# Four edits in an attention-and-feed-forward kernel: spare matmuls ahead of the first transposes, column-index steps moved, a group's work moved, one batch's second product taken by halves

## The chip, the cores and the metric

The kernel runs on one NeuronCore of one Trainium2 chip. The metric is the device time of one execution in microseconds (us). The kernel before takes 352.08 us (median of 3 runs, 351.84 to 352.71).

Names of engines, as the profile has them: PE is the matrix engine and PEld its weight load; DVE, ACT and POOL are the vector, scalar and general engines; SP is a queue that here only issues DMAs. POOL issues DMAs too. Each engine and each queue works through its own list in order; semaphores order them against each other.

## What is computed

```python
# attention: q, k, v of (8 batches, 8 heads, 576 tokens, 64), 8 global tokens, window 32
scores = 1/sqrt(D) * q @ k.T
mask = abs(i - j) <= 32  or  i is global  or  j is global
attn = softmax(where(mask, scores, -1e9))
x = attn @ v                      # -> (4608, 512)
# feed-forward with 2048 hidden columns
h = x @ w_in
g = h + sin(alpha * h)**2 / (alpha + 1e-9)
out = g @ w_out                   # (4608, 512), float32
```

## The kernel before

The eight batches go through three stages, which overlap. **Attention** of batch b (`attention_first` for b = 0, `attention` for the others) takes the four pairs of heads `hp` in turn: scores into the PSUM tile `ring` (L843, L975), exponential on ACT into `E` (L850, L984), mask on DVE (L851, L985), then two products on PE, the sums of the weights (`OB` or `ones`) and the weighted values (`VD` or `VX`), at L882 or L1013; ACT makes the inverse `R` of the sums, DVE multiplies into `xT` (L901, L1031). **gemm1** of batch b makes 16 groups `nt` of 128 hidden columns: eight matmuls with `w_in` (L1172) into one of three PSUM tiles `zn`, `zr`, `zd`, sine on ACT (L1211), square on ACT or DVE (L1214, L1216), and the sum into `H` on DVE (L1217). **gemm2** multiplies `H` by `w_out` (L1266) in blocks of 128 tokens, 16 matmuls to a block, into the two PSUM tiles `zo`; ACT copies each block out and SP stores it. gemm2 of batch b is a generator: `fill(n)` takes its next n matmuls and puts them on PE between the instructions of attention b+1 and of gemm1 of batch b+1 (tables `START`, `FIRST`, `SECOND`, `PER_GROUP` and so on). So the order on each engine is written out by hand, and PE's matmuls run in that order whatever is ready.

Names that the steps below use:

- `turn_part` (L625) transposes the first keys and queries, loaded into parts of `H2` (shown as `H`), by matmuls of 48 columns into `zn`, `zd`, `zo`; `place_part` copies them to `KD` (ACT) and `QX` (DVE). `warm(z, n)` (L576) puts n matmuls of 512 columns of ones on PE whose result is not read.
- `load_lying` (L458) loads keys and queries of batch 1 as they lie, in four DMAs of POOL; `turn_lying` (L733) transposes them in thirds at groups 2, 6 and 9 of gemm1 of batch 0 into both `zo` tiles, and `place_lying` copies them out one group later (DVE to `KX`, L741; ACT to `QX`, L747).
- `turn_kq` (L773, L777) turns the global rows of all batches (`gq`, `gk`, loaded by SP's gathers, L518) into `kTg` and `qTg`, by way of the same `zo` tile. `cast_globals_v` (L765, POOL) makes `VGb` from the gathered `gv`; `place_globals` puts global columns into batch 1's `KX` and `QX`; `load_vg` (L422) and `load_v` (L418) are SP's loads of batch 1's values into `VX`.
- `find_columns` (L1231 to L1243) is seven DVE instructions on 8 or 16 numbers: from the global indices it makes the column numbers `gcol`. They are read in attention 5 by `load_columns`.
- `beside(at)` is called after pair `at` of an attention and holds its side work: `place` (L362, L369), DVE copies of the next batch's keys and queries, and, from batch 2 to batch 5 at pair 2, `pace` (L347), which holds POOL until the first pair's `xT` stands, and then POOL's casting loads of the batch after next (`cast_qk`, L336, and `cast_v`, L343).

Of the kernel before, what the change touches and what calls it, by code (L numbers as in the profile page):

```python
# [249 lines left out]
def kernel(  # L250
# [12 lines left out]
    B, H, S, D = q.shape  # L263
# [8 lines left out]
    NT = DFF // P  # L272
# [72 lines left out]
    def pace(src):  # L345

        nc.gpsimd.tensor_copy(out=seen[0 : src.shape[0]], in_=src)  # L347
# [117 lines left out]
    zo = [banks.tile([P, 512], DT.float32, name=f"zo{i}") for i in range(2)]  # L465
# [108 lines left out]
    def warm(z, n):  # L574
        for _ in range(n):
            nc.tensor.matmul(  # L576
                out=z[:], lhsT=ones[:], rhs=ones[:][:, None, :].to_broadcast([P, 4, P]),
                start=True, stop=True, skip_group_check=True,
            )
# [41 lines left out]
    def turn_part(w, half, z):  # L621
        part[w, half] = z
        rows = slice(D * half, D * half + HK)
        for a in range(NH):
            nc.tensor.transpose(  # L625
                out=z[a // 12][:, a % 12], in_=nat[w][rows, a * P : (a + 1) * P], identity=identb[rows, rows]
            )

    def views(zs):
        return [z.bitcast(DT.bfloat16)[:, 0 : NH // 2 * HK].rearrange("p (a c) -> p a c", c=HK) for z in zs]  # L630
# [32 lines left out]
    def place_global_queries(t, copy):  # L663
        for y in range(2):
# [4 lines left out]
                ].to_broadcast([D, NHP, 7, 4]),  # L669
            )  # L670

    turn_part(1, 0, views([zn[:, n, :] for n in range(2)]))
    for n in range(2):
        place_part(1, 0, n, act)
    turn_part(0, 0, views([zd[:, n, :] for n in range(2)]))

    gpf = setup.tile([P, 1], DT.float32, name="gpf")
    nc.vector.tensor_copy(out=gpf[:], in_=gp64[:].bitcast(DT.int32)[:, 0:1])
# [110 lines left out]
    def halves(z, W):  # L789
        c = columns(z, W)  # L790
        return [(c[:, lo:hi], lo, hi) for lo, hi in ((0, HALF), (HALF, W))]
# [281 lines left out]
    def global_rows(bs):  # L1073

        nc.vector.reciprocal(out=GR[:, :, :, bs], in_=GD[:, :, :, bs])
# [78 lines left out]
    def gemm1(b):  # L1154


        while len(waiting) > 1:
            fill(1)
        xT = xTs[b]
        r0 = (b % 2) * S  # L1160
        more = b == B - 1
        W = SG if more else S
        hr = tc.alloc_tile_pool(name="hr", bufs=1, space=PSUM)
        hs = {}

        def chunks(nt, cs, parts=slice(0, 2)):
            if nt not in hs:
                hs[nt] = (zn, None, zd)[nt % 3] or hr.tile([P, 2, 512], DT.float32, name="zr")
            h = hs[nt]
            for c in cs:  # L1170
                for h_part, lo, hi in halves(h, W)[parts]:
                    nc.tensor.matmul(  # L1172
                        out=h_part, lhsT=w_in[:, c, nt * P : (nt + 1) * P], rhs=xT[:, c, lo:hi],
                        start=(c == 0), stop=(c == CT - 1), skip_group_check=True,
                    )

        on_act = (ON_ACT_FIRST, ON_ACT_SECOND, ON_ACT)[min(b, 2)]
        for nt in range(NT):
            at_group[0] = (b, nt)
            if b == 1 and nt in (10, 12):  # L1180
                for which, t, y in PLACES[nt - 6 : nt - 4]:
                    place(2, which, t, y, nc.vector.tensor_copy)
            if b == 0 and nt in (3, 7, 10):
                for w, copy in ((1, nc.vector.tensor_copy), (0, nc.scalar.copy)):
                    place_lying(w, (3, 7, 10).index(nt), copy)
            if b == 0 and nt == 4:
                turn_kq()
            if b == 0 and nt == 5:

                cast_globals_v()  # L1190
                for part in range(3):
                    place_globals(1, part, nc.gpsimd.tensor_copy)
                load_vg(1)
                load_v(1)
            if more and nt == SOON:
                put_globals(slice(0, SOON))
            if nt == 0:

                for n in range(2):
                    chunks(n, range(CT - 1), slice(0, 2 - more))  # L1200
                for n in range(2 * more):
                    chunks(n, range(CT - 1), slice(1, 2))
            chunks(nt, range(CT - 1, CT) if nt < 2 else range(CT))
            h = columns(hs[nt], W)
            fill((GROUP_LAST if more else PER_GROUP)[nt])
            if nt and copied[0] == (b, nt - 2):
                fill(AFTER_COPY)
            if b == 0 and nt in (2, 6, 9):
                turn_lying((2, 6, 9).index(nt))
            sb = spool.tile([P, SG], DT.bfloat16, name="sb")  # L1210
            nc.scalar.activation(out=sb[:, 0:W], in_=h, func=AF.Sin, scale=alphaT[:, nt : nt + 1])  # L1211
            s2 = spool.tile([P, SG], DT.bfloat16, name="s2")
            if nt in on_act:
                nc.scalar.activation(out=s2[:, 0:W], in_=sb[:, 0:W], func=AF.Square)  # L1214
            else:
                nc.vector.tensor_tensor(out=s2[:, 0:W], in0=sb[:, 0:W], in1=sb[:, 0:W], op=ALU.mult)  # L1216
            nc.vector.scalar_tensor_tensor(  # L1217
                out=H2[:, nt, r0 : r0 + W], in0=s2[:, 0:W], scalar=recipT[:, nt : nt + 1], in1=h,
                op0=ALU.mult, op1=ALU.add,
            )  # L1220
        hr.release()
        at_group[0] = None
# [27 lines left out]
    SOON = 11  # L1250
# [7 lines left out]
    def gemm2(b):  # L1258
        lo, hi = (0, 4) if b % 2 == 0 else (4, 9)

        def bank(blk):
            return zo[(blk + b // 2) % 2]

        def products(blk, ops, nts, cols):
            for nt in nts:
                nc.tensor.matmul(  # L1266
                    out=ops[:, cols], lhsT=H2[:, nt, blk * P : (blk + 1) * P], rhs=w_out[:, nt, cols],
                    start=(nt == 0), stop=(nt == NT - 1), skip_group_check=True,
                )
                yield True  # L1270

        def keep(blk, ops, osb, cols):
            nc.scalar.copy(out=osb[:, cols], in_=ops[:, cols])  # L1273
            copied[0] = at_group[0]
            store(b, blk, osb, cols)

        full = slice(0, DM)
        if b == B - 1:
            for blk in (lo, lo + 1):
                yield from products(blk, bank(blk), range(SOON), full)  # L1280
        for blk in range(lo, hi):
            osb = osbp.tile([P, DM], DT.float32, name="osb")
            if (b, blk) == (B - 1, hi - 1):
                for part, ops in enumerate((bank(blk), zd[:, 1])):
                    cols = slice(part * DM // 2, (part + 1) * DM // 2)
                    yield from products(blk, ops, range(NT), cols)
                    keep(blk, ops, osb, cols)
            else:
                begun = SOON if b == B - 1 and blk < lo + 2 else 0
                yield from products(blk, bank(blk), range(begun, NT), full)  # L1290
                keep(blk, bank(blk), osb, full)

# [33 lines left out]
    def fill(n):  # L1326
        while n and waiting:
            if next(waiting[0], None) is None:
                waiting.pop(0)
            else:  # L1330
                n -= 1
# [15 lines left out]
    def phase_a(b_att, b_moe):  # L1347
        def beside(at):

            if b_moe is None:  # L1350
                if at == 0:
                    second_half()
                    gather(v, gv)
                if at == 2:
                    find_columns()
                if at == NHP:
                    for half in range(2):
                        rows = slice(half * D, (half + 1) * D)
                        nc.sync.dma_start(out=MASKT[rows], in_=MASK[rows, half * NT6 : (half + 1) * NT6])
                return  # L1360
            if at == 2 and b_att == B - 1:
                global_rows(slice(0, B - 1))
            if b_att == 5 and at == 3:
                load_columns()
            if 0 <= at < 2:
                square_x(b_moe, at)
            if at == 2 and 1 < b_att and b_att + 2 < B:
                pace(xTs[b_att][0:1, 0, 0:1])
                cast_qk(b_att + 2)
                cast_v(b_att + 2)  # L1370
            if b_moe == 0 and at == 1:
                turn_qk(2)
            for which, t, y in places_at(b_att, at):
                place(b_att + 1, which, t, y, nc.vector.tensor_copy)

        if b_moe is not None:
            waiting.append(gemm2(b_moe))
        attention(b_att, beside)
# [71 lines left out]
```

## Time and profile before

| | |
|---|---|
| median of 3 runs | 352.08 us (351.84 to 352.71) |
| span of the profiled execution | 351.6 us |
| PE busy | 324.5 us (92%) |
| ACT busy | 287.1 us (82%) |
| DVE busy | 276.1 us (79%) |
| POOL busy | 60.7 us (17%) |
| read and written in HBM | 41.97 MB, 20.77 MB |

All times inside the kernel are read from that one execution, counted from its start; its span stands 0.5 us under the median of the runs. A row of the timeline is: start, length, engine, line, operation, output and inputs, count of equal instructions, and in brackets how long the engine was idle before it and what ended the wait. A row of the windows gives, for a stretch of time, the busy time of each engine, the granted clock of PE as a share of full speed, the mean busy share of the 16 DMA engines as the page's own sum has it, and GB/s. PE's clock is known from the first change that the profile records, at 25.5 us; before that the column prints 1.00, and the lengths of the matmuls tell the clock.

### The profile page before, as it was taken

The numbers are of one execution on the slowest core, as the hardware profiler recorded it, in microseconds if no ns is written. First come the engines' busy times: TensorE is split into PE (matmuls) and PEld (weight loads), VectorE is DVE, ScalarE is ACT, GpSimd is POOL, SyncE is SP. The second block draws the span as 40 slices with busy tenths as digits, with TensorE's granted clock in tenths as the row PEclk, the third lists the DMA queues.
The fourth block names the chain that finished last, engine by engine and source line by source line (L and its number), as shares of the span: only waits on it lengthen the run. The fifth ranks groups of instructions, "written<-read, shape, count | busy, mean of one in ns | idle before, by whom it ended". The sixth has DMA issues, their size and how long they took to land.

```text
span 351.6 us, 10962 instructions
## 1 busy us (share of the span) xinstructions
PE 324.5 (92%) x4484; PEld 207.1 (59%) x4484; DVE 276.1 (79%) x537; ACT 287.1 (82%) x428; POOL 60.7 (17%) x93
## 2 busy tenths in 40 slices
PE   1576798999899999999999999999999999999994
PEld 1566575566645675567656674577556755566543
DVE  6787668778879887987878887978788878788970
ACT  6786778998979888988898888988898787887921
POOL 7966130024004000310003000400000000002510
PEclk9998889999999999999999999999999999999998
DMA  7999999479998957399428936799125011100142
GB/s 113 110 125 171 184 215 232 100 155 170 211 125 170 194 107 164 70 182 216 63 64 167 167 75 146 145 194 185 32 53 134 3 33 64 34 27 5 31 106 66
DMA packets 87762, 42.25 MB, mean 120 GB/s; under 512 B 72378, under 2 KB 82362, under 8 KB 87322
## 3 DMA queue, kind: packets, MB, share of 16 engines
q0 software_dynamic: 44944, 18.52, 44.1%
q1 hardware_dynamic: 42762, 22.98, 30.3%
q8 instruction: 36, 0.59, 0.7%
q14 instruction: 20, 0.16, 0.2%
HBM read 41.97 MB, written 20.77 MB: 178 GB/s over the span
## 4 chain that ended last, share of the span: by engine, by line
PE 43%; issue 29%; DVE 5%; ACT 3%; POOL 2%; POOLq 1%; DVEq 0%; ACTq 0%
PE zo L1266 21%; PE zn L1172 6%; PE zr L1172 5%; PE zd L1172 4%; PE ring L975 3%; DVE H L1217 2%; POOL H L1256 2%; PE zd L1013 2%; PE zn L1013 1%; POOLq L1248 1%; ACT sb L1211 1%; DVE xT L1031 1%; ACT s L1214 1%; DVE KD L369 1%; PE zd L1266 1%
## 5 line engine op out<-in xcount | busy, mean ns | idle before, releaser
L1266 PE MATMUL zo<-w_out,H 128*128 128x512 bf16 (+1 forms) x576 | 149.4, 377 | 0.2 <-POOL H L1256 0.2
L1172 PEld LDWEIGHTS <-w_in 128*128 128x128 bf16 x1024 | 99.8, 98 | 43.0 <-issue 8.2
L1266 PEld LDWEIGHTS <-H 128*128 128x128 bf16 x592 | 52.4, 98 | 44.3 <-POOL H L1256 0.7
L1172 PE MATMUL zn<-xT,w_in 128*128 128x288 bf16 (+1 forms) x384 | 57.3, 288 | 1.7 <-DVE H L1217 1.7
L1172 PE MATMUL zr<-xT,w_in 128*128 128x288 bf16 x320 | 48.7, 291 | 1.5 <-DVE H L1217 1.5
L984 ACT ACTIVATE E<-ring 128x720 bf16<-128x720 f32 x56 | 43.5, 776 | 7.6 <-PE ring L975 6.8
L1211 ACT ACTIVATE sb<-zn,alphaT 128x576 bf16<-128x576 f32 (+1 forms) x48 | 35.7, 743 | 15.2 <-PE zn L1172 15.2
L1217 DVE SCALAR_TENSOR_TENSOR H<-s,recipT,zn 128x576 bf16<-128x576 bf16 (+1 forms) x48 | 39.4, 821 | 9.5 <-ACT s L1214 6.2
L1172 PE MATMUL zd<-xT,w_in 128*128 128x288 bf16 x320 | 46.6, 289 | 0.2
L985 DVE TENSOR_TENSOR E<-E,MASKT 128x720 bf16<-128x720 bf16 x56 | 29.6, 529 | 16.2 <-ACT E L984 16.0
L1214 ACT ACTIVATE s<-sb 128x576 bf16<-128x576 bf16 (+1 forms) x58 | 40.0, 689 | 1.8
L1216 DVE TENSOR_TENSOR s<-sb 128x576 bf16<-128x576 bf16 (+1 forms) x70 | 32.0, 458 | 10.0 <-ACT sb L1211 9.6
L1217 DVE SCALAR_TENSOR_TENSOR H<-s,recipT,zd 128x576 bf16<-128x576 bf16 (+1 forms) x40 | 32.9, 822 | 8.4 <-ACT s L1214 4.4
L1217 DVE SCALAR_TENSOR_TENSOR H<-s,recipT,zr 128x576 bf16<-128x576 bf16 (+1 forms) x40 | 32.9, 822 | 6.5 <-ACT s L1214 5.0
L1211 ACT ACTIVATE sb<-zr,alphaT 128x576 bf16<-128x576 f32 (+1 forms) x40 | 29.7, 743 | 8.3 <-PE zr L1172 8.2
L1211 ACT ACTIVATE sb<-zd,alphaT 128x576 bf16<-128x576 f32 (+1 forms) x40 | 29.5, 738 | 4.8 <-PE zd L1172 4.3
L1273 ACT COPY osb<-zo 128x512 f32<-128x512 f32 (+1 forms) x36 | 20.7, 576 | 8.7 <-PE zo L1266 5.1
L824 ACT ACTIVATE R<-L,shift 128x576 f32<-128x576 f32 x32 | 24.8, 776 | 0.6
L1256 POOL COPY H<-H 128x11 bf16 (+1 forms) x16 | 7.2, 450 | 100.6 <-DVE H L1217 99.8
L347 POOL COPY seen<-xT 1x1 bf16<-1x1 bf16 x4 | 1.6, 405 | 127.6 <-DVE GN L801 127.6
L1031 DVE TENSOR_TENSOR xT<-zn,R 128x576 bf16<-128x576 f32 x21 | 15.8, 753 | 0.7 <-PE zn L1013 0.5
L343 POOL DMA_DIRECT2D vd<-in_v_dram x7 | 16.4, 2337 | 0.1
(181 smaller groups left out, 369.1 us busy)
## 6 DMA issues: line engine op xcount, KB each, us to landing
vd<-in_v_dram POOLq DMA_DIRECT2D x7, 576.0 KB, 16.1
kd<-in_k_dram POOLq DMA_DIRECT2D x6, 576.0 KB, 8.6
qd<-in_q_dram POOLq DMA_DIRECT2D x6, 576.0 KB, 10.5
VX<-vd SPq DMA_DIRECT2D x16, 168.0 KB
w_in<-in_moe_w_in_dram POOLq DMA_DIRECT2D x4, 512.0 KB, 8.7
w_out<-in_moe_w_out_dram POOLq DMA_DIRECT2D x4, 512.0 KB, 23.3
VD<-vd SPq DMA_DIRECT2D x12, 168.0 KB
out_dram<-osb SPq DMA_DIRECT2D x7, 256.0 KB
```

Source lines behind the costliest of these rows:

```text
L343: nc.gpsimd.dma_start(out=cast[b, "vd"][:], in_=v[b].rearrange("h s d -> s h d"))
L824: nc.scalar.activation(out=R[:], in_=L[:], func=AF.Exp, scale=-1.0, bias=shift[:, 0:1])
L984: nc.scalar.activation(out=Eg, in_=zs[:, :, 0 : G3 * WCOL], func=AF.Exp, scale=scale)
L985: nc.vector.tensor_tensor(out=Eg, in0=Eg, in1=MASKT[:, None, G3 * g : G3 * (g + 1), :].rearrange("p o m c -> p o (m c)").to_broadcast([P, ...
L1031: nc.vector.tensor_tensor(out=xT[:, hp, 0:S].rearrange("p (k m c) -> p k m c", k=4, c=KT), in0=tokens(nd(hp, 0)), in1=Rs[hp][:], op=ALU.mult,)
L1172: nc.tensor.matmul(out=h_part, lhsT=w_in[:, c, nt * P : (nt + 1) * P], rhs=xT[:, c, lo:hi], start=(c == 0), stop=(c == CT - 1), skip_group ...
L1211: nc.scalar.activation(out=sb[:, 0:W], in_=h, func=AF.Sin, scale=alphaT[:, nt : nt + 1])
L1214: nc.scalar.activation(out=s2[:, 0:W], in_=sb[:, 0:W], func=AF.Square)
L1216: nc.vector.tensor_tensor(out=s2[:, 0:W], in0=sb[:, 0:W], in1=sb[:, 0:W], op=ALU.mult)
L1217: nc.vector.scalar_tensor_tensor(out=H2[:, nt, r0 : r0 + W], in0=s2[:, 0:W], scalar=recipT[:, nt : nt + 1], in1=h, op0=ALU.mult, op1=ALU.add,)
L1266: nc.tensor.matmul(out=ops[:, cols], lhsT=H2[:, nt, blk * P : (blk + 1) * P], rhs=w_out[:, nt, cols], start=(nt == 0), stop=(nt == NT - 1) ...
L1273: nc.scalar.copy(out=osb[:, cols], in_=ops[:, cols])
```

## The change

Four edits, no arithmetic changed:

1. `warm` puts 12 spare matmuls ahead of the first transposes of keys, 5 between these and the transposes of queries, and 12 behind them: 29 of 128x512 in all, into `zo[0]`.
2. `find_columns` goes from pair 2 of attention 0 to pair 2 of attention 3, ahead of `pace` and `place`.
3. In gemm1 of batch 0, `turn_kq` goes from ahead of group 4 to ahead of group 5; `cast_globals_v`, `place_globals`, `load_vg(1)` and `load_v(1)` go from group 5 to group 6.
4. gemm2 of batch 0 takes the first 8 of the 16 matmuls of block 0, the first 8 of block 1, the last 8 of block 0, the last 8 of block 1, and then blocks 2 and 3 as before.

```diff
+    warm(zo[0], 12)
     turn_part(1, 0, views([zn[:, n, :] for n in range(2)]))
     for n in range(2):
         place_part(1, 0, n, act)
+    warm(zo[0], 5)
     turn_part(0, 0, views([zd[:, n, :] for n in range(2)]))
+    warm(zo[0], 12)
...
-            if b == 0 and nt == 4:
+            if b == 0 and nt == 5:
                 turn_kq()
-            if b == 0 and nt == 5:
+            if b == 0 and nt == 6:
 
                 cast_globals_v()
                 for part in range(3):
...
         full = slice(0, DM)
-        if b == B - 1:
-            for blk in (lo, lo + 1):
-                yield from products(blk, bank(blk), range(SOON), full)
+        ahead = {0: NT // 2, B - 1: SOON}.get(b, 0)
+        for blk in (lo, lo + 1):
+            yield from products(blk, bank(blk), range(ahead), full)
...
-                begun = SOON if b == B - 1 and blk < lo + 2 else 0
+                begun = ahead if blk < lo + 2 else 0
                 yield from products(blk, bank(blk), range(begun, NT), full)
                 keep(blk, bank(blk), osb, full)
...
                 if at == 0:
                     second_half()
                     gather(v, gv)
-                if at == 2:
-                    find_columns()
...
             if at == 2 and b_att == B - 1:
                 global_rows(slice(0, B - 1))
+            if b_att == 3 and at == 2:
+                find_columns()
```

The order on DVE in gemm1 of batch 0, where group 3's `H` (L1217 before, L1220 in the change; `zn` is its PSUM tile) and group 4's (`zr`) stand around the two casts of `turn_kq`. Before:

```order
L741 COPY KX_94<-zo_125 128x48x2x8
L1217 SCALAR_TENSOR_TENSOR H_97<-s_883,recipT,zn 128x576
L777 CAST kTg<-zo_125 128x256
L777 CAST qTg<-zo_125 128x256
L1216 TENSOR_TENSOR s_907<-sb 128x576
L1217 SCALAR_TENSOR_TENSOR H_97<-s_907,recipT,zr 128x576
```

And in the change:

```order
L744 COPY KX_94<-zo_125 128x48x2x8
L1220 SCALAR_TENSOR_TENSOR H_97<-s_903,recipT,zn 128x576
L1219 TENSOR_TENSOR s_917<-sb 128x576
L1220 SCALAR_TENSOR_TENSOR H_97<-s_917,recipT,zr 128x576
L780 CAST kTg<-zo_125 128x256
L780 CAST qTg<-zo_125 128x256
```

The casts stand one group further from the copy `KX<-zo` that empties the PSUM tile which they and the transposes before them use.

The order on DVE in attention 3, around the end of pair 2: the reductions of pair 1's sums (`GD`), the side work, and the mask of pair 3's first scores (`E`). Before:

```order
L985 TENSOR_TENSOR E<-E,MASKT 128x2x360
L801 TENSOR_REDUCE GD<-zd 128x2x4
L369 COPY KD<-kt 64x48x24 x3
L985 TENSOR_TENSOR E<-E,MASKT 128x2x360
L1031 TENSOR_TENSOR xT<-zn,R 128x576
L801 TENSOR_REDUCE GN<-zn 128x2x4
```

And in the change:

```order
L804 TENSOR_REDUCE GD<-zd 128x2x4
L1234 COPY ci<-girow 1x8
L1235 TENSOR_SCALAR ci<-ci 1x8
L1236 CAST cf<-ci 1x16
L1237 TENSOR_SCALAR cf<-cf 1x8
L1240 SCALAR_TENSOR_TENSOR cf<-cf 1x8
L1243 SCALAR_TENSOR_TENSOR cf<-cf 1x8
L1246 TENSOR_SCALAR gcol<-cf 1x8
L369 COPY KD<-kt 64x48x24 x3
L988 TENSOR_TENSOR E<-E,MASKT 128x2x360
L1034 TENSOR_TENSOR xT<-zn,R 128x576
```

The seven small instructions stand ahead of the three copies, the mask and the `xT` of pair 1.

The order of SP's DMAs from the mask's copy on (`VX` is batch 1's values, `out_dram` the store of a gemm2 block, `LC` a check value of attention 1, `kt` and `qt` the turned keys and queries of batch 2). Before:

```order
L1359 DMA MASKT<-MASK 64x720 x2
L422 DMA VX_93<-VGb 8x7x512 x2
L418 DMA VX_93<-vd 24x7x512 x4
L1299 DMA out_dram<-osb 128x512
L819 DMA LC<-L 2x576
L353 DMA_TRANSPOSE kt<-kd 128x2304
```

And in the change:

```order
L1360 DMA MASKT<-MASK 64x720 x2
L422 DMA VX_93<-VGb 8x7x512 x2
L418 DMA VX_93<-vd 24x7x512 x4
L822 DMA LC<-L 2x576
L1302 DMA out_dram<-osb 128x512
L353 DMA_TRANSPOSE kt<-kd 128x2304
```

Up to the loads of `VX` the queue is as it was; behind them the first store and the check value change places, since block 0 is finished 8 matmuls later.

## The prediction

> **What bounds the kernel now.** I read the windows first, for who is busy when; then the timeline of the first 70 us engine by engine; then the DMA queues; then attention 3, where one edit lands.
>
> ```profile
> core 0: us, PE busy (x) PEld busy (x) DVE busy (x) ACT busy (x) POOL busy (x), PEclk, DMA share, GB/s
> 30.00:60.00 30.00, 24.18 (x372) 18.14 (x371) 22.47 (x42) 21.68 (x35) 7.07 (x11) 0.89 1.35 208
> 60.00:80.00 20.00, 19.93 (x410) 11.32 (x410) 15.52 (x31) 18.21 (x28) 3.00 (x5) 1.00 0.57 130
> 100.00:340.00 240.00, 239.04 (x3296) 147.01 (x3295) 196.90 (x357) 205.75 (x296) 23.32 (x33) 1.00 0.61 104
> ```
>
> From 60 us on PE has no gaps worth the name: 19.93 of 20 us, 239.04 of 240. What PE loses there is lost at the end, and a microsecond gained earlier reaches the end if PE can start its dense stretch earlier. The early part is where PE waits, and there the change works:
>
> ```profile
> 29.24 1.91 DVE L1231 COPY ci<-girow 1x8 int32<-1x8 int32 x1
> 32.41 1.03 DVE L851 TENSOR_TENSOR E<-E,MASK 128x480 bf16<-128x480 bf16 x3
> 28.44 1.58 ACT L850 ACTIVATE E<-ring 128x480 bf16<-128x480 f32 x3
> 32.85 1.33 PE L882 MATMUL zr<-E,OB 128*128 128x88 bf16 x14 [2.60 <-DVE E L851]
> 38.48 0.70 PE L733 MATMUL zo<-identb,H 48*64 48x48 bf16 x64
> 42.49 1.09 PE L773 MATMUL zo<-idf,H 64*128 64x64 f32 x8 [1.78 <-DVE KX L741]
> 45.66 0.74 ACT L1211 ACTIVATE sb<-zr,alphaT 128x576 bf16<-128x576 f32 x1 [3.45 <-PE zr L1172]
> ```
>
> Two stalls of batch 0. DVE spends 29.24 to 32.41 on `find_columns` while the last pair's exponentials, ready from about 29 to 30.02, wait for their mask; PE waits 2.60 us for that. Later `turn_kq` stands on PE behind DVE's copy out of the same PSUM tile, PE stops 1.78 us, and ACT goes without work for 3.45.
>
> **The change part by part.**
>
> *Column steps out of attention 0.* The three masks can then end near 30.4 (behind the exponential that ends at 30.02), and PE's product starts near 30.3 instead of 32.85: 2.5 us earlier, and all of gemm1 of batch 0 behind it.
>
> *The lying keys stop part of that.* The first `turn_lying`, at 38.48, needs the last of four loads:
>
> ```profile
> 26.58 0.59 POOL L458 DMA_DIRECT2D H<-in_q_dram  x1 [0.84 <-DMA w_in<-in_moe_w_in_dram]
> H<-in_q_dram POOLq DMA_DIRECT2D x1, 288.0 KB, 10.1
> ```
>
> It lands at 26.58 + 10.1 = 36.7, and no compute stands before its issue. So this point moves from 38.48 to 36.7: 1.8 us of the 2.5 remain.
>
> *`turn_kq` a group later.* By group 5 the copy is long done: the 1.78 us go, and so does most of what follows (PE's clock is halved just then, below). ACT's whole idle time of 3.45 is the price; its casts still take their time on DVE, but a group later. Sum at the end of gemm1 of batch 0: 1.8 + 3.4 = 5.2 us early.
>
> *Spare matmuls.* PE is idle before the first transposes (6.43 us) and here:
>
> ```profile
> 12.56 0.26 PE L702 MATMUL pg<-identb,g0k 64*64 64x64 bf16 x1 [2.75 <-DMA g0k<-in_k_dram,grow]
> 24.35 0.63 PE L576 MATMUL zo<-ones 128*128 128x512 bf16 x1
> 60.19 2.76 PE L1266 MATMUL zo<-w_out,H 128*128 128x512 bf16 x12
> ```
>
> At full clock one costs about 2.76 / 12 = 0.23 us, at the half clock that the 0.63 of the one at 24.35 shows about 0.46. Twelve behind the second transposes (which end at 9.81, 2.75 before 12.56) take 2.8 or 5.5 us, so the next ones start on time or 2.8 us late. A warm PE gains at most a microsecond or so of setup. Both ends vanish in the wait for the lying keys at 36.7 if they are no more than 0.7 late; beyond that they eat into the 5.2 us, which the next point has to spare. I take 0.
>
> *gemm2 by halves* only matters if batch 0's product starts before the last quarter of `w_out`; it removes a wait that the earlier start would make, and adds no matmul. 0.
>
> *Batch 1's values.* This is where the 5.2 us end. `VX` is first read by PE at 67.72:
>
> ```profile
> 46.79 0.61 POOL L765 CAST VGb<-H 64x512 bf16<-64x512 f32 x1 [8.76 <-DMA LC<-L]
> 48.95 1.70 SPq L418 DMA_DIRECT2D VX<-vd  x4
> 64.78 0.37 SPq L1299 DMA_DIRECT2D out_dram<-osb  x1
> 67.72 0.48 PE L1013 MATMUL zn<-E,VX 56*64 56x88 bf16 x28
> q1 hardware_dynamic: 777, 0.74, 20.3%
> q1 hardware_dynamic: 213, 0.32, 46.5%
> q1 hardware_dynamic: 2, 0.00, 0.6%
> ```
>
> The q1 rows are SP's queue from 50.66 to 64.7, to 66.6, and to 67.6. Between the loads of `VX` (issued from 48.95, 4 x 168 KB) and the store at 64.78 SP issues nothing, so the 0.74 MB up to 64.7 are `VX`, from `vd` and, in small part, from `VGb`; behind it 0.32 MB still go, more than the store's 256 KB; after 66.6 nothing. `VX` is complete between 64.7 and 66.6, and I take 66.6. Its issue hangs on SP's order and on `VGb`, which waits for the gathers of `gv` (the row names `LC`, the queue's next): DMAs throughout, and the change moves none of them ahead (`load_v(1)` is only written a group later; SP's row of DMAs up to it is the same). So PE arrives at 67.7 - 5.2 = 62.5 and waits to 66.6. Of 5.2 us, 67.7 - 66.6 = **1.1** reach the dense stretch; with 64.7 it would be 3.0.
>
> *The clock after that wait.* A wait of 4.1 us is not free here:
>
> ```profile
> 28.95:32.37 3.42, 1.21 (x19) 0.98 (x18) 3.21 (x8) 2.38 (x5) 2.78 (x2) 1.00 0.95 178
> 32.37:35.78 3.41, 2.93 (x31) 2.73 (x32) 2.52 (x10) 1.51 (x3) 0.77 (x2) 0.50 1.10 194
> 42.60:46.02 3.42, 3.42 (x19) 2.42 (x20) 1.32 (x3) 0.36 (x1) 0.00 (x0) 0.50 1.80 183
> 93.81:97.22 3.41, 2.28 (x16) 1.55 (x16) 3.23 (x7) 3.24 (x6) 0.00 (x0) 1.00 1.86 214
> ```
>
> The granted clock changes on a grid of 3.41 us: a stretch with PE busy 1.21 of 3.42 is followed by one at 0.50, one with 2.28 of 3.41 is not. Laid over that grid, an idle 4.1 us always leaves one stretch with under 1.4 busy. So at least one dense stretch at half clock follows: 3.41 / 2 = **1.7 us** lost; two of them, 2.6, where the wait ends inside the slow one; 0 if the threshold lies lower than 1.2. [...]
>
> *Column steps into attention 3.* There PE is the bound and DVE has no slack to speak of:
>
> ```profile
> 148.31 2.23 POOL L343 DMA_DIRECT2D vd<-in_v_dram  x1
> 147.22 1.38 DVE L369 COPY KD<-kt 64x1152 bf16<-64x1152 bf16 x3
> 148.63 0.53 DVE L985 TENSOR_TENSOR E<-E,MASKT 128x720 bf16<-128x720 bf16 x1
> 149.75 0.22 DVE L801 TENSOR_REDUCE GN<-zn 128x8 f32<-128x64 f32 x1
> 150.41 0.50 PE L1013 MATMUL zn<-E,VX 56*64 56x88 bf16 x28
> 152.00 0.76 DVE L1031 TENSOR_TENSOR xT<-zn,R 128x576 bf16<-128x576 f32 x1
> 152.99 0.91 PE L1172 MATMUL zn<-xT,w_in 128*128 128x288 bf16 x6
> 77.18 2.23 POOL L343 DMA_DIRECT2D vd<-in_v_dram  x1
> 78.33 1.87 DVE L369 COPY KD<-kt 64x1152 bf16<-64x1152 bf16 x2
> 28.72 2.25 POOL L343 DMA_DIRECT2D vd<-in_v_dram  x1
> ```
>
> The seven take 32.41 - 29.24 = 3.17 in attention 0, of which the first 1.91; behind it 1.26. The three `KD` copies at 147.22, which now stand behind them, take 0.46 each; but two of the same kind at 78.33, inside POOL's `vd` issue, took 1.87 instead of 0.92, and the copy of 29.24, inside the one of 28.72, ended at 31.15, 0.18 behind that issue's end. So a DVE copy in SBUF that starts inside a `vd` issue ends with it. In attention 3 the issue runs 148.31 to 150.54. Now the three copies start before it; behind the seven (0.17 + 1.26 = 1.4) the first starts at 148.6, inside it. Then it ends near 150.9, the three at 151.8, the mask of 148.63 starts 3.1 us late, and so does all behind it on DVE. PE at 150.41 needs `zn` free, which the `GN` of 149.75 does at 149.97: 0.44 of slack, so 2.7 are lost there; gemm1 of batch 3 (152.99) needs the `xT` of 152.00 and starts **3.0** late. Without the hold it is 1.4 - 0.44 = 1.0 at the first point and 1.3 at the second.
>
> *Sum* against the profiled execution: 351.6 - 1.1 + 1.7 + 3.0 = 355.2. The median of the runs stands 0.5 above its span: **355.7 us**, slower by 1.0%.
>
> **The rivals.**
>
> *The hold doesn't happen* (for it: DVE copies inside other POOL issues were not lengthened; against: both copies that started inside a `vd` issue were): 355.7 - 1.7 = 354.0, and without a slow stretch behind the `VX` wait 352.3.
>
> *`VX` is not the limit* (for it: the loads share the engines with casts that could drain differently, and their end is bounded only to 64.7; against: nothing ahead of them in the queues moves). All 5.2 us arrive, no cold stretch: 352.1 - 5.2 + 3.0 = 349.9 with the hold, 348.2 without: the faster side. It decides if `VX` stands by 63 or so.
>
> *The edits cancel*: with `VX` at 64.7 (3.0 gained, a wait of 2.2 that the clock survives) and the hold 352.1, no change.
>
> *A second slow window and a second hold*: the idle of 2.7 in attention 3 cools PE too (up to 1.7), or batch 2's transposed loads, which come earlier, put POOL's `vd` issues under attention 1's `KD` copies (up to 2): 357.4 to 358.
>
> **How the numbers follow.** Forecast (hold, `VX` wait, with its cold stretch or with the extra of the last rival) 0.55; hold absent 0.18; `VX` not the limit 0.17; cancelling 0.10. The forecast's own range is 354.3 to 358. The whole range, 350.0 to 358.0, leaves out most of the faster rival's 349.9 and 348.2 and little above. About 0.3% (1.06 us) is what a measurement can tell from no change. Slower by more: the forecast and most of the hold-absent case with its cold stretch, 0.66; same: the cancelling case and 352.3, 0.15; faster 0.19.
>
> **What would show it.** In the changed profile: PE's `zr` product near 30.3 or earlier; `turn_lying` starting at a load's landing near 36.7; no PE wait at L776; PE waiting on a `VX` load at its first L1016 product with `VX`, ending near 66.6, and a window at 0.50 behind; in attention 3 a `KD` copy of some 2 us and PE idle 2 to 3 us. If PE reads `VX` before 64 us, or DVE's copies in attention 3 keep 0.46 us, the forecast is wrong.

## The result, and the profile after

The changed kernel is slower: 356.55 us median of 20 runs (353.22 to 360.32) against 352.56 us of the kernel before (20 runs, 350.98 to 355.07). The ratio is 1.0074, 95% interval 1.005 to 1.0099; it leaves out seven runs of the changed kernel that lie over 1.5% above its fastest (the other thirteen have a median of 355.04), so it is smaller than the quotient of the medians, 1.011.

The profiled execution has a span of 357.0 us and took 358.75, which is in the upper half of the twenty. A second profile of the same kernel (358.0 us, span 356.3) was taken among the experiments. The two lose their time by partly different ways, so both are shown. In the change's file line numbers are 3 higher than before from L676 to L1353 of before (L1016 was L1013, L1220 was L1217).

The windows of the first profile, the stretches of which the prediction shows those of before:

```profile
30.00:60.00 30.00, 24.79 (x391) 18.30 (x389) 21.23 (x37) 23.49 (x37) 6.73 (x11) 0.94 1.35 204
60.00:80.00 20.00, 17.77 (x387) 10.54 (x391) 14.62 (x29) 16.64 (x26) 4.62 (x5) 1.00 0.62 132
100.00:340.00 240.00, 229.63 (x3223) 145.15 (x3263) 196.20 (x359) 205.01 (x295) 23.10 (x33) 1.00 0.58 102
```

Up to 60 us PE is better off: 24.79 us busy instead of 24.18, at a clock of 0.94 instead of 0.89. From 60 to 80 us it has lost 2.2 us of the 19.93 it had. In the last stretch 9.4 us of busy time seem to be gone, but part of that is missing records (73 matmuls fewer than before, 3223 against 3296), so the ledger below goes by the start of instructions.

First the timeline of the first profile, the rows at which the prediction's steps and the ledger stand:

```profile
30.38 0.79 PE L885 MATMUL zr<-E,OB 128*128 128x88 bf16 x14
33.99 1.31 PE L885 MATMUL zd<-E,VD 128*128 128x88 bf16 x14 [2.82 <-DMA VD<-VG]
38.94 0.70 PE L736 MATMUL zo<-identb,H 48*64 48x48 bf16 x64
42.95 0.86 PE L776 MATMUL zo<-idf,H 64*128 64x64 f32 x8 [0.80 <-DVE KX L744]
65.93 0.21 PE L1016 MATMUL zn<-E,VX 56*64 56x88 bf16 x2
67.67 0.49 PE L1016 MATMUL zn<-E,VX 56*64 56x88 bf16 x26 [1.53 <-DMA VX<-vd]
71.14 0.80 ACT L987 ACTIVATE E<-ring 128x720 bf16<-128x720 f32 x1
78.16 3.15 DVE L369 COPY KD<-kt 64x1152 bf16<-64x1152 bf16 x2
78.21 2.82 POOL L343 DMA_DIRECT2D vd<-in_v_dram  x1
82.78 1.14 PE L1175 MATMUL zn<-xT,w_in 128*128 128x288 bf16 x8 [1.58 <-DVE H L1220]
148.76 0.77 ACT L827 ACTIVATE R<-L,shift 128x576 f32<-128x576 f32 x1
149.44 2.43 POOL L343 DMA_DIRECT2D vd<-in_v_dram  x1
149.65 2.97 DVE L369 COPY KD<-kt 64x1152 bf16<-64x1152 bf16 x3
154.03 0.48 PE L1016 MATMUL zn<-E,VX 56*64 56x88 bf16 x25 [2.43 <-DVE GN L804]
156.95 0.90 PE L1175 MATMUL zn<-xT,w_in 128*128 128x288 bf16 x6 [0.27 <-DVE GN L804]
234.30 0.41 PE L1175 MATMUL zn<-xT,w_in 128*128 128x288 bf16 x2
```

Then the timeline of the second profile of the same kernel:

```profile
30.30 0.79 PE L885 MATMUL zr<-E,OB 128*128 128x88 bf16 x14
35.45 0.70 PE L736 MATMUL zo<-identb,H 48*64 48x48 bf16 x64
39.46 0.91 PE L776 MATMUL zo<-idf,H 64*128 64x64 f32 x8 [0.80 <-DVE KX L744]
62.60 0.21 PE L1016 MATMUL zn<-E,VX 56*64 56x88 bf16 x2
65.88 0.49 PE L1016 MATMUL zn<-E,VX 56*64 56x88 bf16 x26 [3.08 <-DMA VX<-vd]
70.71 0.77 ACT L987 ACTIVATE E<-ring 128x720 bf16<-128x720 f32 x1 [1.06 <-PE ring L978]
146.84 0.77 ACT L827 ACTIVATE R<-L,shift 128x576 f32<-128x576 f32 x1
147.50 2.43 POOL L343 DMA_DIRECT2D vd<-in_v_dram  x1
147.72 2.96 DVE L369 COPY KD<-kt 64x1152 bf16<-64x1152 bf16 x3
152.10 0.48 PE L1016 MATMUL zn<-E,VX 56*64 56x88 bf16 x25 [2.43 <-DVE GN L804]
156.25 0.91 PE L1175 MATMUL zn<-xT,w_in 128*128 128x288 bf16 x6
233.16 0.77 PE L1175 MATMUL zr<-xT,w_in 128*128 128x288 bf16 x5 [0.85 <-issue]
233.78 0.41 PE L1175 MATMUL zn<-xT,w_in 128*128 128x288 bf16 x2
```

And its windows on the grid on which the granted clock changes (the last three columns are the clock, the DMA share and GB/s):

```profile
63.82:67.23 3.41, 1.35 (x30) 0.72 (x30) 1.79 (x5) 0.83 (x2) 0.00 (x0) 1.00 0.78 199
67.23:70.64 3.41, 3.41 (x73) 1.93 (x74) 0.92 (x4) 1.79 (x3) 0.00 (x0) 0.50 1.23 233
149.15:152.56 3.41, 0.98 (x43) 0.59 (x45) 3.37 (x7) 1.11 (x2) 0.79 (x1) 1.00 1.08 189
152.56:155.97 3.41, 3.41 (x53) 1.41 (x43) 2.45 (x7) 2.71 (x3) 0.00 (x0) 0.50 1.21 187
```

The ledger compares the start of the same instruction; the rows of before that the prediction does not show are these, from its timeline:

```profile
71.22 0.80 ACT L984 ACTIVATE E<-ring 128x720 bf16<-128x720 f32 x1
147.64 0.77 ACT L824 ACTIVATE R<-L,shift 128x576 f32<-128x576 f32 x1
229.51 0.41 PE L1172 MATMUL zn<-xT,w_in 128*128 128x288 bf16 x2
```

| point | before | first profile | second profile | predicted |
|---|---|---|---|---|
| PE reaches batch 1's `VX` | 67.72 | 65.93 (-1.8) | 62.60 (-5.1) | -5.2 |
| PE goes on with `VX` | 67.72 | 67.67 (-0.1) | 65.88 (-1.8) | -1.1 |
| an exponential behind it | 71.22 | 71.14 (-0.1) | 70.71 (-0.5) | +0.6 |
| attention 3, ahead of the copies | 147.64 | 148.76 (+1.1) | 146.84 (-0.8) | +0.6 |
| gemm1 of batch 3 | 152.99 | 156.95 (+4.0) | 156.25 (+3.3) | +3.6 |
| gemm1 of batch 5, a later group | 229.51 | 234.30 (+4.8) | 233.78 (+4.3) | +3.6 |
| end | 351.6 | 357.0 (+5.4) | 356.3 (+4.7) | +3.6 |

How to read it: in the second profile 5.1 us are gained, 3.1 wait for a load, 1.3 go in the slow stretch behind the wait, and attention 3 takes 4.1 (from -0.8 to +3.3): some 2.7 by the held copies, 1.4 by a second slow stretch, the one at 152.56. In the first profile a wait for `VD` at 33.99 takes the gain of the column steps at once, `VX` takes the rest, attention 1 loses 1.2 by a held copy at 78.6, and attention 3 loses 2.8 without a slow stretch. Some 1.4 us more go behind 157 us in both: 0.8 and 1.0 in the first products of gemm1 of batch 5, where PE stops without a recorded reason, and 0.36 in gemm1 of batch 6 (the last section has both).

### The profile page after: what moved, and what is told of

It is laid out like the page before. It is cut to its first block, busy times and chain, and to the rows that moved or that the text cites. A ratio compares the mean times of both kernels' runs of the same rounds, so it can differ in the third digit from the quotient of the medians.

```text
span 357.0 us, 10964 instructions
## 1 busy us (share of the span) xinstructions
PE 324.5 (91%) x4456; PEld 208.4 (58%) x4513; DVE 277.0 (78%) x537; ACT 286.7 (80%) x428; POOL 61.4 (17%) x93
## 4 chain that ended last, share of the span: by engine, by line
PE 37%; issue 31%; DMA 9%; DVE 8%; ACT 7%; POOL 3%; POOLq 1%; SPq 1%; another core or an unknown queue 1%; DVEq 0%; ACTq 0%
PE zo L1269 16%; PE zn L1175 6%; PE zr L1175 5%; DMA VX<-vd 4%; PE zd L1175 4%; DMA VD<-VG 3%; DVE H L1220 2%; PE ring L978 2%; POOL H L1259 2%; DMA LC<-L 2%; DVE KD L369 2%; ACT KD L641 2%; ACT sb L1214 1%; DVE xT L1034 1%; PE zn L1016 1%
## 5 line engine op out<-in xcount | busy, mean ns | idle before, releaser
L1269 PE MATMUL zo<-w_out,H 128*128 128x512 bf16 (+1 forms) x519 | 135.4, 376 | 6.3 <-issue 5.6
L1220 DVE SCALAR_TENSOR_TENSOR H<-s,recipT,zn 128x576 bf16<-128x576 bf16 (+1 forms) x48 | 39.4, 821 | 10.6 <-ACT s L1217 7.0
L1217 ACT ACTIVATE s<-sb 128x576 bf16<-128x576 bf16 (+1 forms) x58 | 40.0, 689 | 1.8
L1220 DVE SCALAR_TENSOR_TENSOR H<-s,recipT,zd 128x576 bf16<-128x576 bf16 (+1 forms) x40 | 32.9, 822 | 8.4 <-ACT s L1217 5.3
L1220 DVE SCALAR_TENSOR_TENSOR H<-s,recipT,zr 128x576 bf16<-128x576 bf16 (+1 forms) x40 | 32.9, 821 | 6.5 <-ACT s L1217 5.0
```

The costliest lines, as they stand in the source:

```text
L1220: nc.vector.scalar_tensor_tensor(out=H2[:, nt, r0 : r0 + W], in0=s2[:, 0:W], scalar=recipT[:, nt : nt + 1], in1=h, op0=ALU.mult, op1=ALU.add,)
L1269: nc.tensor.matmul(out=ops[:, cols], lhsT=H2[:, nt, blk * P : (blk + 1) * P], rhs=w_out[:, nt, cols], start=(nt == 0), stop=(nt == NT - 1) ...
```

## The experiments

All timed runs stand beside runs of the kernel before on the same chip (352.6 to 353.0 median).

**1. Column steps back in attention 0.** The changed kernel with one edit undone:

```diff
             if b_moe is None:
                 if at == 0:
                     second_half()
                     gather(v, gv)
+                if at == 2:
+                    find_columns()
...
-            if b_att == 3 and at == 2:
-                find_columns()
```

> The changed kernel with one edit undone: the column-index steps stand in attention 0 again. Theory (attention 3 loses 2.8 us because the KD copies fall inside POOL's vd issue, and the gain in attention 0 is eaten before batch 1's numerators by the wait for VX): the three KD copies near 149 us take 1.4 us again instead of 2.97, PE's wait of 2.4 us on GN at 154 is gone, PE still waits for VX near 67, and the time is 2.8 us under the changed kernel: about 353.7. Rival (the column steps in attention 0 were worth their 2.5 us and the loss is elsewhere): slower than or like the changed kernel, 356.5 to 359.

350.80 us; ratio to before 0.9959 (0.9928 to 0.9991). From its timeline, attention 3:

```profile
145.01 1.38 DVE L369 COPY KD<-kt 64x1152 bf16<-64x1152 bf16 x3
146.10 2.23 POOL L343 DMA_DIRECT2D vd<-in_v_dram  x1
```

The copies take 0.46 each, PE has no wait there. So the loss sits in this edit, and it is larger than the theory said: 5.7 us of median, or some 4 us by the two ratios (1.0074 and 0.9959). Without it the other three edits make the kernel 0.4% faster. In this profile PE came to `VX` at 65.27 and lost only 0.47 there, so that part of the theory was hardly tested.

**2. Column steps alone.** The kernel before with only this move:

```diff
-                if at == 2:
-                    find_columns()
...
+            if b_att == 3 and at == 2:
+                find_columns()
```

> The kernel before with this one edit: the column-index steps moved from attention 0 to attention 3. Theory: 2.8 us lost in attention 3 by held KD copies; in attention 0 the zr product starts near 30.3, PE reaches VX up to 1.8 us early and waits for it, so at most 0.1 us reach batch 1; batch 2's transposed loads come up to 1.6 us earlier and put POOL's second vd issue over attention 1's KD copies, which costs a further 1.2: 355.3 to 356.5. Rival (attention 0's gain reaches the end): 352.5 - 2.5 + 2.8 = 352.8 or less.

357.06 us; ratio 1.0135 (1.0094 to 1.0176). The copies took 2.96 us again and PE stopped 2.43; the windows of this run behind it:

```profile
148.70:152.12 3.42, 0.99 (x45) 0.60 (x47) 3.38 (x7) 1.09 (x2) 0.76 (x1) 1.00 1.01 183
152.12:155.53 3.41, 3.41 (x52) 1.41 (x44) 2.41 (x7) 2.71 (x3) 0.00 (x0) 0.50 1.22 188
```

The wait leaves a window with 0.99 us busy, and the next one runs at half clock: 1.4 us (the same instructions are 1.4 late at 151.3 and 2.8 late at 154.9). That is the part by which the estimate, 355.3 to 356.5, was too low. The part in attention 1 did not happen in this profile (two copies 1.87, as before). Without gemm2 by halves PE stopped 2.83 us for `w_out` at 60.96 and then found `VX` ready at 65.97, 1.75 us before the kernel before reads it: the wait changed its place, and some of the gain passed `VX` (1.3 us at 140 us).

**3. Global rows a group later, alone.** In the kernel before:

```diff
-            if b == 0 and nt == 4:
+            if b == 0 and nt == 5:
                 turn_kq()
-            if b == 0 and nt == 5:
+            if b == 0 and nt == 6:

                 cast_globals_v()
```

> The kernel before with this one edit: the global rows turned at group 5 of batch 0's gemm1 instead of 4, and the casts that follow at group 6. Theory: PE's stall of 1.78 on KX shrinks to 0.8 or less, gemm1 of batch 0 ends about 1.8 us early, PE then waits 1.5 us for VX and starts its product with it near 67.7 as before, so nothing of it is kept; attention 1's KD copies may fall under the second vd issue (+1.2): 352.5 to 353.8. Rival (VX is not the limit): 352.5 - 1.8 = 350.7.

352.59 us; ratio 1.0001 (0.9972 to 1.0031). The time is the theory's, the reason is not shown: in the profile of this kernel PE came to `VX` at 66.00, 1.7 us early, and found it there. That execution took 351.87, below its median.

**4. Spare matmuls alone.** In the kernel before:

```diff
+    warm(zo[0], 12)
     turn_part(1, 0, views([zn[:, n, :] for n in range(2)]))
     for n in range(2):
         place_part(1, 0, n, act)
+    warm(zo[0], 5)
     turn_part(0, 0, views([zd[:, n, :] for n in range(2)]))
+    warm(zo[0], 12)
```

> The kernel before with only the spare matmuls ahead of the first transposes. Theory: PE's clock is full from about 6 to 16 us, the transposes take 0.6 to 0.8 instead of 1.14, but the first scores wait for ACT's copies and start near 16.0 as before: no change, 352.5 within 0.7. Rival (a warm PE shortens the setup): 351.5 or less.

353.31 us; ratio 1.0032 (1.0012 to 1.0052). The transposes took 0.77 instead of 1.14 us as expected, and nothing of it is left at 37 us. Slower by 0.3% rather than equal; its profile (span 351.8) doesn't show by what.

**5. Column steps where DVE is idle.** The changed kernel with `find_columns` at the end of attention 0:

```diff
                 if at == NHP:
+                    find_columns()
                     for half in range(2):
...
-            if b_att == 3 and at == 2:
-                find_columns()
```

> The changed kernel with the column-index steps at the end of attention 0, behind the last xT, where DVE was idle 2.4 us before gemm1's first group. Theory (the loss of the edit is the hold of the KD copies in attention 3 and the cold clock that can follow it; its gain in attention 0 ends in waits for loads): no held copy at 149, no wait on GN, the zr product near 30.4, and about the time of the kernel with the steps back in attention 0, 350 to 351.5. Rival (the 2.5 us of attention 0 reach the end once attention 3 is free): 348.3.

352.39 us; ratio 0.9968 (0.9938 to 0.9997). No copy is held in attention 3. From its timeline, PE at `VX`:

```profile
62.39 0.21 PE L1016 MATMUL zn<-E,VX 56*64 56x88 bf16 x2
65.63 0.49 PE L1016 MATMUL zn<-E,VX 56*64 56x88 bf16 x26 [3.03 <-issue]
```

The row names no releaser, but the last `VX` load is recorded as complete at 65.54. PE comes 5.3 us early, waits 3.0, and a slow stretch of 3.41 us follows (66.03 to 69.44 at 0.50, behind a window with PE busy 0.40 us). So the time saved in attention 0 ends at `VX`, and the kernel is no faster than with the steps left where they were (experiment 1). The rival's 348.3 is not reached.

**6. `VD<-VG` ahead of the gathers of k.** The changed kernel, on SP's list:

```diff
-    gather(k, gk)
...
     load_vg0()
+    gather(k, gk)
     gather(q, gq)
```

> The changed kernel with SP's eight VD<-VG loads issued ahead of the eight row gathers of k instead of behind them. Theory (the changed kernel's runs fall into a group of 353.2 to 355.6 and one of 357.5 to 360.3, and the upper one is the profiled case, where the last VD<-VG load is issued behind POOL's lying loads, lands at 33.85 and makes PE and, by its reused semaphore, SP's gathers wait): the wait of 2.82 us at 34 is gone in every run, the upper group with it, median about 354.7. Rival (the groups come from the clock behind the hold in attention 3, cold in some runs): two groups as before, median 356 to 357.

359.53 us; ratio 1.0157 (1.0113 to 1.0202). The theory fell: the wait for `VD` is gone, but the runs still spread from 355.7 to 362.2, and a new wait appears, since the gathers of q now come last:

```profile
42.48 0.43 PE L776 MATMUL zo<-idf,H 64*128 64x64 f32 x4 [2.61 <-DMA H<-in_q_dram]
```

**7. Column steps one pair earlier in attention 3.** They then stand ahead of the `xT` for which POOL's `pace` waits, instead of behind it:

```diff
-            if b_att == 3 and at == 2:
+            if b_att == 3 and at == 1:
                 find_columns()
```

> The changed kernel with the column-index steps one pair earlier in attention 3, ahead of the xT on which POOL's issue is paced; the same seven instructions in the same attention. Theory (the hold): the vd issue moves with the KD copies, these take 0.46 each again, and only DVE's own 1.3 us are left: 1.5 to 2.8 us under the changed kernel, 353.7 to 355. Rival (it is DVE's time for the steps that costs, not the hold): like the changed kernel, 356 to 357.

353.50 us; ratio to before 0.9989 (0.9955 to 1.0023). From its timeline:

```profile
147.80 1.38 DVE L369 COPY KD<-kt 64x1152 bf16<-64x1152 bf16 x3
148.89 2.23 POOL L343 DMA_DIRECT2D vd<-in_v_dram  x1
```

The same seven instructions in the same attention cost 3 us less, because POOL's issue moves with the copies. In the profile attention 3 loses 1.2 us (from 0.6 early to 0.6 late against the kernel before) instead of 2.8 and 4.1. This is the run that shows the hold: DVE's own time for the steps is still spent, and it is the 1.2.

**8. The changed kernel once more.**

> The changed kernel once more, for a second profile. Theory: if its time is in the lower group (353.2 to 355.6), PE does not wait for VD<-VG near 31 to 34 and the VX loads are issued before 50 us; in both groups the three KD copies near 149 take about 3 us and PE stops 2.4 us there. Rival (the hold is the accident of one run): copies of 0.46 each in a run of the lower group.

357.99 us; its rows are the second profile above. Its time lies in the upper group, its `VX` loads went out at 48.56 and there is no wait for `VD`: the two groups aren't told apart by that. The held copies are in both profiles; the rival asked for a run of the lower group, and there is no profile of one.

**9. `VX` from `vd` issued first.** On the kernel of experiment 5:

```diff
-                load_vg(1)
                 load_v(1)
+                load_vg(1)
```

> The kernel with the column steps at the end of attention 0 (352.39 median; its PE waits 3.0 us for VX, landed at 65.5), with SP's four VX<-vd loads issued ahead of the two VX<-VGb loads. Theory (VX's landing is set by what the DMA engines still have to carry, not by when it is issued): the loads go out up to 1.5 us sooner, land within 0.5 us of 65.5, time 352.4 within 0.8. Rival (the issue sets the landing): VX 1.2 us or more sooner, 351.2 or less.

350.16 us; ratio 0.9921 (0.9891 to 0.9951). The time is the rival's. This run's profile fell on its slowest execution (354.04) and shows half of it: by their semaphores the four loads were complete at 62.37 instead of the 65.54 of experiment 5, but the two from `VGb`, now behind them, only at 65.39, and PE waited for these (1.2 us in all, to 65.48). The profile of experiment 11, which has the same order, shows all six complete at 59.3. The four went out from 46.91 in experiment 5, from 46.54 here and from 45.21 in experiment 11: the sooner they went out, the sooner they were complete, though not by equal steps.

**10. Batch 2's casts held behind `VX`.** On the kernel of experiment 5:

```diff
             if b == 0:
+                nc.gpsimd.tensor_copy(out=seen[D : D + 1], in_=VX[1][D : D + 1, 0, 0, 0:1])
                 cast_qk(2)
```

> The kernel with the column steps at the end of attention 0, with POOL's casts of batch 2's k and q to DRAM held back until the third VX load has landed, so that they don't share the DMA engines with VX. Theory (VX is kept waiting by the casts' packets of 18432 bytes, beside its own of 1024): VX lands before 62, PE's wait of 3.0 us and the slow stretch of 3.41 us behind it go, 4.7 us in all; batch 2's transposed loads come some 3 to 8 us later and give part of it back in attention 1: 348 to 351. Rival (the casts don't matter to VX): VX still at 65 or later and the casts later still: 352.5 to 356.

353.67 us; ratio 1.0052 (1.0019 to 1.0084). From its timeline:

```profile
62.98 0.48 PE L1016 MATMUL zn<-E,VX 56*64 56x88 bf16 x28
73.99 0.92 DVE L369 COPY KD<-kt 64x1152 bf16<-64x1152 bf16 x2 [4.18 <-DMA kt<-kd]
75.87 1.19 PE L1175 MATMUL zn<-xT,w_in 128*128 128x288 bf16 x6 [2.10 <-DVE GN L804]
```

`VX` is there when PE comes, at 62.98 (the last load was complete at 61.24, not at 65.54 as in experiment 5): the casts do keep it waiting. But DVE then stands 4.18 us in front of its `KD` copies, whose transposed keys come late, PE waits behind it (2.10 us) and its clock falls once (at 76.86 six products with `w_in` take 1.65 us instead of 0.90). The theory's reason was right and the sum was not: the time is where the rival put it.

**11. The second `vd` issue of attention 1 later.** On the kernel of experiment 9:

```diff
             cast_qk(3)
-            cast_v(3)
...
             nc.scalar.activation(out=sb[:, 0:W], in_=h, func=AF.Sin, scale=alphaT[:, nt : nt + 1])
+            if (b, nt) == (1, 3):
+                pace(sb[0:1, 0:1])
+                cast_v(3)
```

> The fastest version so far (column steps at the end of attention 0, VX<-vd loads ahead of VX<-VGb; 350.16 median) with POOL's cast of batch 3's v to DRAM, the second vd issue of attention 1, moved behind batch 1's fourth gemm1 group. Theory (in runs in which that issue covers attention 1's last KD copies, as in the profiles where two copies took 3.1 us, PE loses 1.2 us; DVE's other operations are not held, as the 0.46 and 0.81 us ones inside the issue of 79.84 of the kernel before show): no held copy in attention 1, gemm1 of batch 1 undisturbed by the moved issue, 349.0 to 350.0. Rival (the hold in attention 1 costs nothing at the end, or gemm1's operations are held in its place): 350.2 or more.

349.82 us; ratio 0.9916 (0.9886 to 0.9947), which can't be told from experiment 9. From its timeline:

```profile
45.21 1.63 SPq L418 DMA_DIRECT2D VX<-vd  x4
62.74 0.48 PE L1016 MATMUL zn<-E,VX 56*64 56x88 bf16 x28
73.40 2.23 POOL L343 DMA_DIRECT2D vd<-in_v_dram  x1
73.95 2.46 DVE L369 COPY KD<-kt 64x1152 bf16<-64x1152 bf16 x2
```

All 28 products with `VX` start at 62.74 without a wait and without a slow stretch: 5.0 us of gain go past the point where the changed kernel lost them. In attention 1 the other `vd` issue, at 73.40, now holds a copy (2.46 for two), and gemm1 of batch 1 is 0.8 later for it; gemm1's own operations kept their 0.45 and 0.81 us under the moved issue. The theory had no held copy there at all, and since the time can't be told from experiment 9, what the move is worth is not shown.

**12. The order of the `VX` loads alone**, in the kernel before:

```diff
-                load_vg(1)
                 load_v(1)
+                load_vg(1)
```

> The kernel before with only the order of the VX loads turned (VX<-vd ahead of VX<-VGb). Theory (VX is in time there: PE reads it at 67.7, 1 us behind its landing, so an earlier VX is worth nothing until PE comes earlier): 352.6 within 0.7. Rival (the swap is worth its 2 us by itself): 350.6 or less.

352.92 us; ratio 1.0011 (0.999 to 1.0032). By itself the swap is worth nothing, as the theory said: PE starts on `VX` at 67.31 without a wait, and `VX` only limits a PE that comes early.

The kernels of experiments 9 and 11 are faster than both kernels of this study, by 0.8% against the one before.

## Why the prediction was right, and where its steps were off

The time forecast, 355.7, lies 0.9 under the median; the sign and the two main reasons (the wait for `VX`, the held copies) held. How close the number is, is partly luck. The two profiled spans lose 5.4 and 4.7 us, not 3.6, by terms that the sum did not have: a held copy in attention 1 or a second slow stretch, and the stops in batches 5 and 6. The median is nearer to the forecast because both profiles come from the upper half of the runs.

- *Column steps out of attention 0.* `zr` was to start near 30.3 and did at 30.38 and 30.30. Right.
- *The lying keys.* The first `turn_lying` was to wait for a load until 36.7. In the second profile it starts at 35.45 without a wait, 3.0 us early instead of 1.8, so that limit was wrong: the row of before was taken as fixed, and its load moved with POOL's list, which was 1.7 us earlier here. In the first profile another load, `VD<-VG`, stood in the way, which the prediction did not have.
- *`turn_kq` a group later.* The stall was to vanish; 0.80 of 1.78 remain in both profiles, for the copy `KX<-zo` was not long done. The slow stretch at 42.6 did go. So this step gave 2.1 us instead of 3.4. Together with the point before, the sum came out right, 5.1 against 5.2, by two errors that cancel.
- *Spare matmuls, gemm2 by halves.* Taken as 0. The halves were not run by themselves; experiment 2, which lacks them, waits 2.8 us for `w_out` in place of `VX`, as the prediction said. The spare matmuls alone cost 0.3% (experiment 4). The microsecond of setup at most was an estimate: there the transposes took 0.77 instead of 1.14 us, PE's first scores started at 14.33 instead of 16.01, and at the first `turn_lying` nothing of it was left (38.52 against 38.48).
- *Batch 1's values.* The step on which the sign rested. PE was to come at 62.5 and wait to 66.6; it came at 62.60 and waited to 65.88 (65.93 and 67.67 in the first). The reading of 66.6 was right for the kernel before, where the last load's semaphore stands at 66.57, but it was no fixed limit: the loads went out at 48.95 there, at 48.56 in the second profile (complete at 65.79) and at 50.65 in the first (67.58). Experiment 11 confirms it by taking the limit away. The reason given, SP's order, was half of it: the load's end also hangs on the casts that POOL puts beside it (complete at 61.24 with them held back in experiment 10, at 65.54 in experiment 5).
- *The clock after that wait.* One slow stretch for 1.7 us: in the second profile one stretch, 1.3 us, behind a window with 1.35 us busy; none in the first, where PE waited only 1.53 and its window had 1.93 us busy.
- *Column steps into attention 3.* 3.0 late was forecast; 2.8 was measured in the first profile, and 2.7 in the second ahead of its slow stretch, by the copies as said; but the first of the three ran its 0.44 us, though it started 0.2 inside the issue, and it is the second that was held, for 2.04. The mis-sized term is what follows: a stretch at half clock followed the wait, 1.4 us, in three of the four profiles with that held copy (the second here, experiments 2 and 6). The prediction had this only in its last rival, beside a held copy in attention 1, which came in the first profile (1.2 us).

What spreads the changed kernel's 20 runs over 7 us is not settled: both profiles are from their upper half, and experiment 6 speaks against one cause. The mean granted clock goes with it (0.979 to 0.986 in the six shortest runs, 0.968 to 0.978 in the seven longest), so more time at half clock goes with the longer runs; which waits bring it there is not shown.

## What to carry to other kernels

A small piece of work moved off one path is paid for where it lands: look at what its new neighbours overlap with, here a copy that slid by 1.3 us under another engine's DMA issue and then cost twice that. Time gained early is worth what the next load allows, so follow it to the first load that does not move, and move that load first; pushing its competitors back handed the wait to the next reader here (4.18 us on DVE in experiment 10). What a wait on the matrix engine costs in clock is read from the windows around it: the same 2.43 us cost 1.4 more in the second profile, where they left one window with 0.98 us busy, and nothing more in the first, where they lay across two:

```profile
149.38:152.80 3.42, 2.06 (x48) 1.21 (x50) 3.33 (x6) 2.81 (x6) 2.43 (x1) 1.00 1.02 172
152.80:156.21 3.41, 2.02 (x65) 1.25 (x66) 3.32 (x9) 1.26 (x2) 0.00 (x0) 1.00 0.96 177
```

## What the runs showed of the hardware

- Inside a `vd` issue of POOL DVE's copies were held: in the first profile 2.04 and 2.69 us instead of 0.45 (the second copies of the rows at 149.65 and 78.16), in the kernel before 1.37 (the first copy at 78.33), each until 0.2 or 0.3 us behind the issue's end. The copy that started 0.21 us into the issue, at 149.65, was not: 0.44. The first of the column steps in the kernel before, 1.91 us instead of the 0.15 it takes in attention 3, is one of the held. Masks, products and sums that started inside one kept their 0.53, 0.76 and 0.81 us. In experiment 12 an operation with one input and a scalar was held too, the last of the column steps, 1.82 us instead of 0.16, inside the issue from 29.62 to 31.87:

```profile
30.23 1.82 DVE L1243 TENSOR_SCALAR gcol<-cf 1x8 int32<-1x8 f32 x1
```

- The granted clock changed on a grid of 3.41 us: in the kernel before it stood at 0.50 from 32.37 to 35.78 and from 42.60 to 46.02, behind windows with PE busy 1.21 and 1.25 us:

```profile
39.19:42.60 3.41, 1.25 (x9) 0.80 (x10) 3.32 (x6) 2.99 (x6) 0.00 (x0) 1.00 2.06 167
```

  Windows with PE busy 0.98 and 1.35 us (the second profile) and 0.99 (experiment 2) were followed by half clock too; in the first profile these two were not:

```profile
64.05:67.47 3.42, 1.93 (x62) 1.16 (x62) 2.65 (x7) 3.28 (x6) 0.00 (x0) 1.00 0.29 74
81.12:84.53 3.41, 1.83 (x15) 1.33 (x14) 3.17 (x6) 1.10 (x2) 0.00 (x0) 1.00 2.03 241
```

  In the other profiles windows of 1.54, 1.63 and 1.69 us (experiments 3, 4 and 1) were followed by half clock and windows of 1.59 and 1.66 (experiments 2 and 9) were not. So the busy time of a window alone does not tell whether half clock follows: between 1.59 and 1.69 us both were seen.

- In both profiles of the changed kernel and in experiments 1, 6 and 11 PE stops 0.7 to 1.0 us in the first products of gemm1 of batch 5 with no releaser recorded; in the kernel before and in the other eight it does not. What it waits for stays open.
- In gemm1 of batch 6 DVE stands 0.46 us between two operations of its own, where it takes 0.10 before, and 0.36 us are lost to the end. All nine profiles of kernels with the column steps moved have it, experiment 5 too, and none of the five that left them in their place, so it belongs to that edit; how, stays open. From the first profile:

```profile
274.00 0.81 DVE L1220 SCALAR_TENSOR_TENSOR H<-s,recipT,zn 128x576 bf16<-128x576 bf16 x1 [0.46 <-DVE s L1219]
```
